# Fourteen idle matmuls in place of twelve, and a new hand-written order of work, in a kernel that mixes an FFT filter with a two-layer network

## The chip, the cores and the metric

The kernel runs on one core of one Trainium2 chip. The metric is the device time of one execution in microseconds (us). Before the change it is 129.68 us, the median of three runs (129.40, 129.68, 129.87). The engines are called PE or TensorE (matmuls), ACT or ScalarE, DVE or VectorE, POOL or GpSimd, and SP (which issues most DMAs here).

## What is computed

The input x has 2048 rows of 512 values in bf16. Three things are made of it:

```python
g = _sigmoid((x * gate_w).sum(-1, keepdims=True))   # one number for each row
a = irfft2(rfft2(x) * (w_r + 1j * w_i))             # a filter in two-dimensional frequency space
h = x @ w1 + b1                                     # 512 -> 1792
b = (h * tanh(softplus(h))) @ w2                    # Mish, then 1792 -> 512
return g * a + (1 - g) * b
```

The part with w1 and w2 is called the dense part below, the one with the FFT the spectral part.

## The kernel before

**Tasks.** `_build` doesn't loop over work and issue it. It makes a graph of 615 tasks (`G.add`, L175), each with an engine, a function that issues its instructions, what it reads and writes, and the PSUM banks that it takes and frees. `schedule` (L216) then reads the string `ORDER` (L258 to L274), which lists all tasks in one order: two digits in base 62 are a task's number (in the order of creation); where a task may run on several engines a letter chooses one (`v` VectorE, `a` ScalarE, `g` GpSimd); where it takes a PSUM bank one more digit names the bank (of eight). Each engine runs its own tasks in that order (`run_engine`, L842), strictly one after the other, and waits by semaphore for the tasks on other engines that a task depends on. A task that takes a bank depends on everything that read the bank's former content (L236 to L247). The constants in `PR`, the durations such as `mm`, `dve_dur`, `pool_dur` and the `tail` and `bw` of a DMA are the costs by which a planner made the string; when the kernel is built they choose nothing.

**Warm-up.** `warm0` to `warm15` (L423 to L429) are matmuls of a zeroed tile, which nobody reads: the first `NWARM` = 12 have 256 columns, the other `NFILL` = 4 have 128. They are tasks too; thirteen stand in front of the first transposes and three behind.

**Loads.** x comes in five DMAs on SP (`ld_x0`: tiles 0 and 1, `ld_x2`: tiles 2 and 3, then four tiles each). The first block of w1 comes in two halves, `ld_w1_0_0` and `ld_w1_0_1`, on the queue of ScalarE. All DMAs of SP go out in SP's order.

**Transposes.** `tr0a`, `tr0b`, `tr2a`, `tr2b` transpose two tiles of x and half of the columns each (four matmuls of 128 columns, L476), `tr4` to `tr14` two tiles (eight); `evx...` copy the result to xT.

**Dense part.** For each of four chunks of 512 rows (`c`) `mm1_c_ft` (L773, four matmuls of 512 columns) makes one of 14 blocks of h and `mish_c_ft` (ScalarE, L788) applies Mish. The first four blocks of chunk 0 are cut into quarters, `mm1a0_ft`, `mm1a1_ft`, `mm1b0_ft`, `mm1b1_ft`: `a` and `b` are the first and the last 256 rows, 0 and 1 the halves of w1 (two matmuls of 256 columns each). `mm2_t_0` and `mm2_t_1` (L803, seven matmuls of 512 columns each) make row tile t of b, and `bev_t` (L755 on ScalarE, L756 on VectorE) copies it out times 1 - g.

**Spectral part.** `ts`, `td` (VectorE) fold xT, `a10`, `a11` (L512) transform the rows, `eg` (ScalarE) and `e1p`, `e1m`, `e1f` combine, `s1` (L538) transforms the columns, `e2` copies out, `r1w` and `r1r` write it to memory and read it back in another layout. `s2` (L635), `wm` (VectorE), `wz` (GpSimd), `s2i` (L695) multiply by the filter; `e4`, `r2w`, `r2r` copy, write and read back. `s1i_t` (L723), the copy `e5_t` and `a1i_t` (L734; four matmuls of 128 columns each) transform back. From the bank of `a1i_t`, `gc_t` (ScalarE, L739) and then `sam_t` and `sap_t` (VectorE, L745) make sums and differences; these three free the bank. `sbm_t` and `sbp_t` (L751, `tt` at L408) add and subtract them, from SBUF to SBUF, on GpSimd; at the end `sum_t` (VectorE, L823, from SBUF to SBUF, L408 too) adds the dense and the spectral part, and an `out` DMA stores two tiles. Tiles 14 and 15 have `fin_t` (L815) in place of `sum_t`.

**Gate.** `gdot0` to `gdot15` (VectorE, L554), then `gpow` (GpSimd, L559), `gadd`, `gcol`, `omg` (VectorE).

Of the kernel before, what the change touches and what calls it, by code (L numbers as in the profile page):

```python
# [165 lines left out]
class _Graph:  # L166
# [89 lines left out]
DIGITS = "0123456789ABCDEFGHIJKLMNOPQRSTUVWXYZabcdefghijklmnopqrstuvwxyz"  # L256
ENGINE = {"p": "pe", "a": "act", "v": "dve", "g": "pool", "s": "sp"}
ORDER = (  # L258
    "020L0M0T0500O060N070P03080R090A0Q000B040C010S0D0E0F0U0G0V0H2y0w30W0y70I0J0xv0X0K6k50Y6z11046p00Z11a0a0zv1220b6"
    "u313v1G7701H711Jv6l0c6m721Iv6v736w6x6n6y1K40d7420e1M6o1L10f1461Nv750g1630h15v7670i1Ov1U40j1V27717v1850k1Pv0l1e"  # L260
    "v1W7810m1fv0n7A31Xv0o790p1Yv1A67B0q1C10r1Bv1Za1r70s1Dv1g41i0t19v7C20u2i7E37D20v7G62j7F6q21v1q47H1h26r1s1kv6s7I"
    "16t2k1la7K31jv7J2l7M47L1uv2322m7N2252D67a0241vv1tv1E126v7b25v27v7c37e07d1Fv2C72n7f1Q27g12E2Mv7i01Rv7h331a47j2G"
    "v7k11S1ba2Fv7m02Nv1T7l2Hv1m22o1c7n2O62Y71nv1d7o12Q2a2Z02p7q57p1o2cv1p2P11w32Rv7r7s62Sv1xa7u72dv2bv7t1y2822q7v2"
    "I41z29v7w12Ta2Ja2U62r7x2A7y32Vv2B2e17z2K8002s2fa2L8E62t2W818G72u2X8F2v2g8I58H2h2w8K18J2x8L2z8M2388O0398N3A8Q78"
    "P3B8S68R30318U1328T0v8V347358W4368Y2378X8a08Z3C38b3D63E8c53Mv8e18d3F3Qv3G7O08f3Pv7P3Lv3Sg3H23Y67Qa3I3Ng3Z43a7R"
    "23hv3Rg3b7S3c3mv3Og3d17U07Ta3e3J3iv3K3T7V3lv3jg3U43kg7Wa7X13Wa3Vv3ng3X3u63v23og7Y3w44v3f43v3g8s07Za3p3x48v3q44"
    "5g8t8u13sa3rv46g8w08v47v4G43t8x3y4H68y14Tv4Ag3z28208z4Pv49g834J404I4Qv414K424B9014Uv4Sg4L4922914M84v4N4C44Wg93"
    "8514Da4Ev4O4Vg4F864X4Rg94087a4Y4958814Za4av4b898B08Aa8C4c4d4e8g18Da4f963982979A0999C59B4g34o49D9E04hv4pa4i54w3"
    "9F5444q64xv4j8h55a4l4r4k4t5C04ng5K48ia4s4y55625Dv4mg5La5S38j15Tv4z4vg57514ug505E7595a453g5F5i3585U65ba8k5jv52g"
    "5V5G5Bg5X5H8m05Ag8la5W9av9bv5k59ev5M29c5l8n9dv5N5Ig9f5P5Jg5O8p18oa5Zg5m5n5Rg5c25q49gv5y55d6635Qg5ra5zv9G667a5f"  # L270
    "5pg6055e9H9I75Yg615s39hv8q9J635hg9i5t629jv5v5gg6E68ra5u6M49K764g6Nv6Fa9kv5xg9l6816U3699L5og6Vv6A5wg6B6c365g9Ma"
    "6W56G49N09nv6da9pv6H9mv6X6I6Dg9O9o6Z6Y6Cg6J6ag6O76e39Pa9Q29qv6f6bv9r6P6Lg6g6R9R6Kg6Q6h6Tg9U59sv9S6ig6jv9T9X16S"
    "g9V9W9tv9u9Y9Z"
)  # L274
NBF = 14
GD_N = 8
# [6 lines left out]
SPEC = (3, 4, 5, 6, 7)  # L283
DENSE = {0: (0, 1, 2, 3), 1: (0, 1), 2: (0, 1), 3: (0, 1)}
DENSE2 = {0: (0, 1), 1: (0, 1), 2: (0, 1), 3: (0, 1)}
NWARM = 12
NFILL = 4
PR = dict(tr=99.0, sp=95.0, mm1=88.0, mish=97.0, mm2=70.0, fin=98.0, gate=96.9, sum=98.5)

# [1 line left out]
def _build(nc, A_x, A_w_r, A_w_i, B_x, B_w1, B_b1, B_w2, gate_w, out):  # L291
# [8 lines left out]
    with es:  # L300
# [86 lines left out]
        def mm(n):  # L387
            return n / 2400.0 + 0.0025
# [10 lines left out]
        def pe(name, dur, fn, **kw):  # L399
            return G.add(name, "pe", dur, fn, lat=0.17, **kw)  # L400
# [21 lines left out]
        tw = []  # L422
        for i in range(NWARM + NFILL):  # L423
            n = 256 if i < NWARM else 128
            tw.append(pe(f"warm{i}", mm(n), lambda e, n=n: e.matmul(ps[:, pw.bank, 0:n], act[:, 2, 0, 0:128], act[:, 2, 0, 0:n], start=True, stop=True),  # L425
# [512 lines left out]
```

## Time and profile before

| | us |
|---|---|
| median of three runs | 129.68 |
| time of the profiled execution | 130.35 |
| its span, first to last instruction | 128.6 |
| TensorE busy | 123.2 |
| VectorE busy | 90.9 |
| ScalarE busy | 70.9 |
| GpSimd busy | 52.7 |

The difference between the span and the time of the same execution, 1.75 us, lies around the span. Busy time of TensorE has a peculiarity: matmuls are pipelined, so that the duration of one (0.379 us for 512 columns) is longer than the distance to the next (0.216). Where a row counts fewer instructions than the code issues, records are missing, and the profile shows the place as idle time.

### The profile page before, as it was taken

Reading aid. Unit: us, or ns where it says so; the run is one execution under the profiler, and the core shown is the slowest. Engines: PE = TensorE matmul, PEld = TensorE weight load, DVE = VectorE, ACT = ScalarE, POOL = GpSimd, SP = SyncE. Lnnn points to the kernel's source line nnn. Section 1 sums busy time; section 2 is a strip of 40 time slices with the busy share of each in tenths; the row PEclk is TensorE's granted clock in tenths of the full one; section 3 lists DMA queues with packets and bytes.
Section 4 is the critical chain, followed back from the end, with each engine's and each line's share of the span. In section 5 each row is a group of like instructions: output and inputs, shape, how many; then the busy total and the mean of one; then the engine's idle time right before and its main releaser. Section 6 shows DMA issues by size and latency. Waiting matters only on the chain.

```text
span 128.6 us, 2680 instructions
## 1 busy us (share of the span) xinstructions
PE 123.2 (96%) x1012; PEld 68.0 (53%) x1030; DVE 90.9 (71%) x173; ACT 70.9 (55%) x115; POOL 52.7 (41%) x83
## 2 busy tenths in 40 slices
PE   6999999999999999999999999999999999999992
PEld 4787756645544444444444444444466556555571
DVE  0255999998999711987679994300059999889992
ACT  1347768779898877522228415722597536735400
POOL 4000000001000266079897789200008977895770
PEclk9999999999999999999999999999999999999999
DMA  3999999999945559700040500555930012220313
GB/s 76 341 399 398 281 179 194 169 259 353 342 128 155 171 148 382 290 0 0 5 136 28 163 3 15 158 163 138 392 125 0 5 63 100 84 82 22 147 41 122
DMA packets 18509, 20.11 MB, mean 156 GB/s; under 512 B 1216, under 2 KB 15552, under 8 KB 18368
## 3 DMA queue, kind: packets, MB, share of 16 engines
q1 hardware_dynamic: 17648, 19.15, 49.9%
q10 hardware_dynamic: 816, 0.79, 1.9%
q8 instruction: 8, 0.13, 0.4%
q14 instruction: 5, 0.04, 0.1%
q0 software_dynamic: 32, 0.00, 0.0%
HBM read 13.64 MB, written 6.29 MB: 155 GB/s over the span
## 4 chain that ended last, share of the span: by engine, by line
PE 92%; DMA 3%; ACT 2%; issue 1%; DVE 0%
PE ps L773 38%; PE ps L803 37%; PE ps L476 3%; PE ps L723 3%; PE ps L512 3%; PE ps L734 3%; PE ps L538 3%; DMA xo<-in_A_x_dram 3%; ACT act L788 2%; PE ps L635 1%; ACT xo L755 1%; PE ps L695 0%; DVE xo L815 0%; PE ps L425 0%; PE ps L484 0%
## 5 line engine op out<-in xcount | busy, mean ns | idle before, releaser
L773 PE MATMUL ps<-xT,w_sb 128*128 128x512 bf16 (+1 forms) x231 | 52.5, 367 | 0.6 <-issue 0.2
L803 PE MATMUL ps<-w_sb,act 128*128 128x512 bf16 (+1 forms) x229 | 49.4, 366 | 0.9 <-ACT act L788 0.3
L788 ACT ACTIVATE act<-ps,b1f 128x512 bf16<-128x512 f32 x56 | 38.3, 687 | 17.2 <-PE ps L773 12.5
L803 PEld LDWEIGHTS ps<-w_sb,act 128*128 128x128 bf16 x238 | 22.3, 98 | 22.8 <-issue 0.8
L773 PEld LDWEIGHTS ps<-xT,w_sb 128*128 128x128 bf16 x240 | 22.6, 99 | 21.9 <-issue 0.6
L408 POOL TENSOR_TENSOR Tg<-Qb 128x256 bf16<-128x256 f32 x30 | 22.8, 791 | 20.7 <-DVE Qb L745 20.7
L408 POOL TENSOR_TENSOR Zb<-Qb 128x510 bf16<-128x510 f32 x16 | 20.0, 1268 | 4.7 <-DVE Qb L408 3.8
L755 ACT ACTIVATE xo<-ps,omg 128x512 bf16<-128x512 f32 x13 | 8.9, 687 | 22.9 <-PE ps L803 17.5
L408 DVE TENSOR_TENSOR Qb<-ps,WT 128x1024 f32<-128x1024 f32 x16 | 18.8, 1214 | 0.7 <-POOL Zb L408 0.7
L745 DVE SCALAR_TENSOR_TENSOR Qb<-ps,gcol,Qb 128x256 f32<-128x256 f32 x32 | 13.5, 474 | 0.7 <-POOL Tg L408 0.6
L403 DVE CAST Zb<-ps 128x512 bf16<-128x512 f32 x8 | 5.5, 689 | 11.9 <-PE ps L723 11.8
L403 DVE CAST Ybuf<-ps 128x1024 bf16<-128x1024 f32 x8 | 9.8, 1220 | 5.6 <-PE ps L695 5.1
L408 DVE TENSOR_TENSOR Abuf<-ps,Tg 128x512 bf16<-128x512 f32 x16 | 10.5, 682 | 2.1 <-PE ps L512 2.1
L576 POOL COPY wrv<-WT 128x32 bf16<-128x32 bf16 x2 | 0.4, 227 | 26.6 <-DMA WT<-in_A_w_i_dram 26.6
L554 DVE SCALAR_TENSOR_TENSOR Tg<-xo,Tg 128x512 bf16<-128x512 bf16 x16 | 10.9, 684 | 0.2
L739 ACT ACTIVATE Qb<-ps,gcol 128x256 f32<-128x256 f32 x16 | 7.1, 475 | 4.0 <-PE ps L734 4.0
L408 DVE TENSOR_TENSOR xo<-xo,Tg 128x512 bf16<-128x512 bf16 x14 | 9.1, 678 | 0.0
L403 DVE COPY xT<-ps 128x1024 bf16<-128x1024 bf16 (+1 forms) x9 | 5.2, 595 | 5.3 <-PE ps L476 5.3
L559 POOL TENSOR_TENSOR gcol<-omg,gdot 128x16 f32<-128x16 f32 x1 | 2.9, 2942 | 14.5 <-DVE Tg L554 14.5
L404 ACT ACTIVATE Ybuf<-ps 128x1024 bf16<-128x1024 f32 x8 | 8.2, 1021 | 0.1
L734 PE MATMUL ps<-GMs,Zb 128*128 128x128 bf16 x64 | 5.5, 219 | 0.0
L476 PE MATMUL ps<-ident,xo 128*128 128x128 bf16 x64 | 5.4, 236 | 0.1
(61 smaller groups left out, 84.2 us busy)
## 6 DMA issues: line engine op xcount, KB each, us to landing
Abuf<-scr SPq DMA_DIRECT2D x8, 512.0 KB, 5.6
scr<-Ybuf SPq DMA_DIRECT2D x16, 128.0 KB, 2.2
scr<-Ybuf SPq DMA_DIRECT2D x4, 512.0 KB, 2.9
w_sb<-in_B_w_dram SPq DMA_DIRECT2D x2, 896.0 KB, 12.7
out_dram<-xo SPq DMA_DIRECT2D x7, 256.0 KB, 2.0
xo<-in_A_x_dram SPq DMA_DIRECT2D x3, 512.0 KB, 7.6
rt<-c_rt SPq DMA_DIRECT2D x2, 512.0 KB, 8.8
WT<-in_A_w_r_dram SPq DMA_DIRECT2D x7, 128.5 KB, 11.0
```

The lines of the kernel that those rows point to most:

```text
L403: fs = {"dve": ("dve", dve_dur(n, rate=rate), lambda e: e.tensor_copy(out=dst(), in_=src())), "act": ("act", act_dur(n), lambda e: e.activ ...
L404: "act": ("act", act_dur(n), lambda e: e.activation(dst(), src(), AF.Copy))}
L408: f = lambda e: e.tensor_tensor(out=o(), in0=i0(), in1=i1(), op=op)
L476: ins = e.transpose(psb[:, pt.bank, o:o + 128], xo[:, t0 + i, d0:d0 + 255:2], ident[:, :])
L554: lambda e, t=t: e.scalar_tensor_tensor(out=junk, in0=xo[:, t, :], scalar=1.0, in1=gwb, op0=ALU.mult, op1=ALU.mult, accum_out=gdot[:, t:t ...
L734: ins = e.matmul(ps[:, p5.bank, 128 * i:128 * i + 128], TT[:, sl, 2 * par + ri, :], GMs[:, i, :], start=True, stop=True)
L739: lambda e, t=t, sl=sl, p5=p5: e.activation(gC[:, sl, :].rearrange("p (i n) -> p i n", i=2), ps[:, p5.bank, :].rearrange("p (i n) -> p i n ...
L745: lambda e, t=t, sl=sl, p5=p5, o=o, op=op: e.scalar_tensor_tensor(out=st1[:, sl, o::2, :], in0=ps[:, p5.bank, :].rearrange("p (i n) -> p i ...
L755: G.add_multi(f"bev_{t}", [("act", act_dur(512, True), lambda e: e.activation(xo[:, t, :], ps[:, pd.bank, :], AF.Copy, scale=omg[:, t:t + ...
L773: ins = e.matmul(ps[:, pd.bank, cols[0]:cols[1]], w1_sb[:, i, 128 * ft:128 * (ft + 1)], xT[:, i, 512 * c + cols[0]:512 * c + cols[1]], sta ...
L788: lambda e, ft=ft, pd=pd, hb=hb: e.activation(act[:, hb, ft, :], ps[:, pd.bank, :], AF.Mish, bias=b1f[:, ft:ft + 1]),
L803: ins = e.matmul(ps[:, pd.bank, cs_], act[:, hb, ft, 128 * tl:128 * (tl + 1)], w2_sb[:, ft, cs_], start=(ft == 0), stop=(ft == NFT - 1))
```

## The change

`NWARM` goes from 12 to 14 and the string is a new one:

```diff
 ORDER = (
-    "020L0M0T0500O060N070P03080R090A0Q000B040C010S0D0E0F0U0G0V0H2y0w30W0y70I0J0xv0X0K6k50Y6z11046p00Z11a0a0zv1220b6"
...
-    "g9V9W9tv9u9Y9Z"
+    "30020N0O000V0550Q060P070R080T09010A0S030B040C0U0D0E0F0W0G0H0X0I0J0y30Y1070K0Z11v0za0a0L1261406r20b0M15v6m16w51"
...
+    "vv9Z59X9uv9Y9w9a9b"
 )
...
-NWARM = 12
+NWARM = 14
```

There are 617 tasks now, the two new ones idle matmuls of 256 columns. All others are the same tasks with the same instructions, but for 28 copies and additions that have another engine, and for the banks. Read digit by digit, the two strings give these orders at the places that the prediction speaks of.

TensorE at the start, from the end of the warm-up:

```
before: warm11 warm12 tr0a tr0b warm13 warm14 warm15 mm1a0_0 mm1a0_3 tr2a mm1a0_1 tr2b mm1a0_2 tr_small mm1a1_3 ...
after:  warm13 warm14 tr0a tr0b warm15 warm16 tr2a tr2b mm1a0_1 warm17 mm1a0_0 mm1a0_2 tr_small mm1a0_3 mm1a1_2 ...
```

After the transform back has begun (the order after; banks in brackets where they are spoken of):

```
TensorE: s1i_3 a1i_0 a1i_2 a1i_1 mm2_7_1 s1i_4 s1i_5 a1i_3 mm2_8_0 a1i_5[6] mm2_8_1 mm2_9_0 a1i_4[6] s1i_6 s1i_7
         s1i_8 s1i_9 mm2_9_1 a1i_6 a1i_7 s1i_10[6] mm2_10_0
ScalarE: e5_0 e5_1 e5_3 gc_0 gc_1 gc_2 e5_4 gc_3 e5_5 gc_5 gc_4 e5_7 e5_9 bev_9
VectorE: sam_0 sap_1 sam_1 sap_2 sam_2 bev_7 sap_3 sam_3 sap_0 sam_5 sap_5 bev_8 sum_1 sum_0 sum_2 e5_6 sap_4 e5_8
         sam_4 sum_3 sap_7
GpSimd:  sbm_1 sbp_1 sbm_2 sbp_2 sbp_0 sbm_0 sbp_5 sbm_3 sbp_3 sbm_5 sbp_4 sbm_4
```

The same place before:

```
TensorE: a1i_0 s1i_2 s1i_3 a1i_1 mm2_8_1 s1i_4 s1i_5 a1i_2 a1i_3 s1i_6 mm2_9_0 a1i_4[7] s1i_7 s1i_8 a1i_6 mm2_9_1
         mm2_10_0 a1i_8[5] a1i_5 mm2_10_1 mm2_11_0 a1i_7 s1i_9 s1i_10[5]
VectorE: sam_0 sap_0 sam_1 sap_1 e5_4 e5_6 sam_2 sap_2 sam_3 sap_3 e5_8 sap_4 sam_6 sam_4 sap_6 sum_0 sum_1 sum_3
         sum_2 sam_5 sap_5 sap_8 sam_8 sum_4
GpSimd:  sbp_0 sbm_0 sbp_1 sbm_1 sbp_2 sbm_2 sbp_3 sbm_3 sbm_4 sbp_4 sbp_6 sbp_5
```

Elsewhere: `evx0a` goes from VectorE to ScalarE and `evx2a` the other way; `e4_01`, `e4_20` and `e4_30` go to VectorE, `e4_00`, `e4_21` and `e4_31` to ScalarE; on SP `r1w0a` goes in front of `ld_w2_1`, and `out7` in front of `out5`; on GpSimd `gpow` goes behind `wab1` and `wab2`; the `s1` tasks come earlier among the dense blocks (`s1_0` in front of `tr8`, `s1_14` in front of `mm1_1_10`), all of chunk 3's `mm1` comes before `s1i_0`, where blocks 11 to 13 came behind it, and `sbm_14`, `sbm_15` go to VectorE.

More of the change, by code (lines that the diff above doesn't have):

```diff
@@ L258 @@
 ORDER = (
-    "020L0M0T0500O060N070P03080R090A0Q000B040C010S0D0E0F0U0G0V0H2y0w30W0y70I0J0xv0X0K6k50Y6z11046p00Z11a0a0zv1220b6"
[L260 to L272, printed above, removed]
-    "g9V9W9tv9u9Y9Z"
+    "30020N0O000V0550Q060P070R080T09010A0S030B040C0U0D0E0F0W0G0H0X0I0J0y30Y1070K0Z11v0za0a0L1261406r20b0M15v6m16w51"
@@ new lines @@
+    "I07170c13v6x6n1J0d1Kv6y720e731Lv746o0f756s6p1M46q6t1W06z1O6u1N1163701Qv0g1876v0h1Pv7641Y0i19v0j1X17717v0k1av0l"
+    "0m7821Zv0n1gv0o7A0790p1hv1Ra0q7C57B1bv0r0s1S17D0t1A61Tv1t70u1i51s01j40v1k1Bv7E31u1U1mv7G10w7F1wv1V1na1C02k7H7I"
+    "61Dv1xa1lv7J22v1c17K31vv1da23v7M07L1e1E17N1f2l7O21Fv7c52m7P2531G02n7d2447e71Hv262Pv7g67f27v2E47h7i12Ov2G28v2F2"
+    "351o67j2Iv2Q529a2R47k32S1pv2Ja7m07l2Hv1q7o12Uv7n1r2o1y62Va7p2Tv7q01za2p3622A4377r2a3202K62Bv382c2b2217s12La392"
+    "ev2C7u02dv7t2D2W42fv2M7v2g62Xv2N7w12ha7y02q7x2Y8062r7z2Z2s8232i812t2j8G1832u8I08H2v8K38J3A2w8M43B8L2x3C8O72y8N"
@@ new lines @@
+    "3D2z8P0x8Q6318S18R8U48T8W08V3E2328X3F6333Nv8Y17Q03Ov8Z343G7R3Pg3H3Rv3Qg3Sv8a47Sa3a23I8b3b03Ug8c63kv8e73Tg3d8d3"
+    "nv3J58g48f3c3K3jv3e7T63L8h3M3V3ov3mg3W23f73Xa3Yv3lg7U3g3Z3qg3w47Va3x23h45v7W03pg3y46v3i7X3r4Av48g3s47Ya49v7Z14"
+    "7g3ua3tv4Bg7a3z3v4Cg4I37ba4J64Rv8u5404128414L8v4Sv4K42854Wv4Ug4Vv438w34M86a444Tg4N58y28x4O9044D8z4P4Yg92091941"
+    "4Q934Xg4E2959604Ga4Fv4Z986974H4a2999A14ca4bv9C79B4d8749D9E69G59F4e9I09H4f9K74g9J4h889L8A189v8B4i58Cv4q34ja4y28"
+    "D74zv4ra5634k157a5064s58E4l4t4n514u5E34v5M4525Fa5804wg8i553598Fv5Na4xg5A54g5O65B8j5P4m55g5R4pg5Q8l18kv4og9dv9c"
@@ L274 @@
+    "v5G65U49fv5H5c55k05Vv5Tg5s35da8m5I5ta5Cg5lv5Dg5J5W45e28na5Sg6069e8o05f9gv61a5Lg5g9h5X5h5Kg5u55Z5m66825v5Y5ig8p"
+    "5n69v5bg5w5o5jg8r15p8qa5x5ag9mv6G58s9lv6Ha5rg9n9iv6O75qg6I28ta6269M05zg6Pa639jv9ov9k6W1655yg6e36A46Xa646Q59N6B"
+    "9pv6R66g9q6D6J6C67g6fa6Y66S9P79Oa6T6Eg6L6Z6Vg6b6g56Fg6a9Q6h9rv6i6dg6K9S49sv9Rv6Ug9t6j9T6cv6kv6lv6Mg9W39U6Ng9V9"
+    "vv9Z59X9uv9Y9w9a9b"
 )
```

## Prediction

> **What bounds the kernel now.** I read the page's busy line and its chain first, then TensorE in order of time, then stretch by stretch.
>
> ```profile
> PE 123.2 (96%) x1012; PEld 68.0 (53%) x1030; DVE 90.9 (71%) x173; ACT 70.9 (55%) x115; POOL 52.7 (41%) x83
> ...
> PE 92%; DMA 3%; ACT 2%; issue 1%; DVE 0%
> ```
>
> TensorE is busy for 96% of the span and is 92% of the chain. Busy is not the same as unstalled, so I compared starts: a 512-column matmul starts 0.216 us after the one before, a 128-column one 0.056. From 7.6 to 126.1 us the starts follow each other at these steps, with 18 holes of 0.216 (or a little more), each of one matmul. The code issues 208 matmuls of 512 columns at L773 and 210 at L803; the rows by shape hold 199 and 201. So the 18 holes are missing records, and the chain's small ACT shares beside them are no waits. **After its start TensorE never waits**; each piece of work it has must be done, so the only thing a new order can win is in the first 7.6 us, and any new wait is paid in full.
>
> TensorE in order of time over the start (start, duration, instructions):
>
> ```profile
> 1.25 2.85 PE L425 MATMUL ps<-act 128*128 128x256 bf16 x13 [1.25 <-DVE act L417]
> 4.19 1.03 PE L476 MATMUL ps<-ident,xo 128*128 128x128 bf16 x8
> 5.02 0.53 PE L425 MATMUL ps<-act 128*128 128x128 bf16 x3
> ...
> 6.94 0.39 PE L476 MATMUL ps<-ident,xo 128*128 128x128 bf16 x4
> ```
>
> Eight transposes take 1.03 us from 4.19, four take 0.39 from 6.94 (each time with 0.16 to 0.21 of tail): the step is 0.107 in the first and 0.056 in the second. Between 6.62 and 6.83 TensorE goes from half rate to full; the page's PEclk row reads 9 throughout and doesn't show it. The first two tiles of x land at 4.14, the next two at 5.51, the second half of the first w1 block at 7.09.
>
> VectorE and GpSimd, at the first final additions (`sum_t`, L823) and the GpSimd additions (`sbm_t`, `sbp_t`, L751):
>
> ```profile
> 102.83 0.73 POOL L408 TENSOR_TENSOR Tg<-Qb 128x256 bf16<-128x256 f32 x1
> ...
> 102.88 2.70 DVE L408 TENSOR_TENSOR xo<-xo,Tg 128x512 bf16<-128x512 bf16 x3
> ...
> 103.52 1.77 POOL L408 TENSOR_TENSOR Tg<-Qb 128x256 bf16<-128x256 f32 x2
> ```
>
> Three sums take 2.70, 0.96 for the first and 0.87 to each further end; a sum with GpSimd idle takes 0.41 (minimum of its row). Each ends about 0.28 after the GpSimd addition under which it began: GpSimd ends at 103.56, 104.43, 105.29, the sums at 103.84, 104.71, 105.58. The two engines take turns, **0.87 a pair**.
>
> **The change, part by part.**
>
> *Two more idle matmuls.* At half rate a 256-column one takes 0.213. The warm-up ends at 3.89 now and would end at 3.89 + 2 x 0.213 = 4.32; the first transpose starts at 4.19 now: 0.13 later. Then eight transposes to 5.17 and two fillers to 5.38, and the second transposes (`tr2a`), moved in front of the first dense blocks, wait for 5.51 + 0.04 = 5.55: 0.17 idle, still at half rate. Eight transposes to 6.41, `mm1a0_1` over the change of rate to 6.78, one filler 0.06, four matmuls of 0.109 to 7.27, `tr_small` 0.21, two of 0.109: 7.70 when the same work is done that now ends at 7.59. **+0.11.** If x lands later than 4.32, or the full rate comes so early that both orders wait for w1 at 7.09, it is nothing; the other end is 0.2 (0.13 + half of 0.17).
>
> *Where the new order makes TensorE wait.* `s1i_10` takes bank 6, which `a1i_4` held, so it waits for the last reader, `sam_4` on VectorE. In VectorE's new queue, behind `bev_8`, stand `sum_1`, `sum_0`, `sum_2`, `e5_6`, `sap_4`, `e5_8`, `sam_4`. I count from the start of the last matmul of `mm2_8_1`, which `bev_8` waits for.
> TensorE up to `s1i_10`: that matmul and the 14 of `mm2_9_0` and `mm2_9_1`, 15 x 0.216 = 3.24; seven tasks of four (`a1i_4`, `s1i_6` to `s1i_9`, `a1i_6`, `a1i_7`), 28 x 0.056 = 1.56; it is free at **4.80**.
> VectorE: the result comes after 0.38, hand-over 0.03: `bev_8` starts at 0.41 and lasts 0.74 (row L756); the next instruction of this engine starts 0.08 before the end of one: 1.07. After the sums, `e5_6` and `e5_8` step by 0.61 (rows of 0.69), `sap_4` by 0.40, `sam_4` lasts 0.47, hand-over 0.04: 2.13 in all. With free sums, 3 x 0.34: 1.07 + 1.02 + 2.13 = 4.22, no wait.
> But GpSimd is then at work. Its first addition waits for `sam_1`. By the same counting back (25 x 0.056 + 20 x 0.216 = 5.71 from `a1i_0` to zero, then `e5_3` 0.60 and `gc_0` 0.47 on ScalarE, three VectorE steps) `sam_1` ends at -3.40, GpSimd begins at -3.37 and steps by 0.69 through ten additions whose inputs are there: the seventh runs 0.75 to 1.48, three more are queued. So `sum_1` ends at 1.48 + 0.28 = 1.76, `sum_0` at 2.63, `sum_2` at 3.50; less the 0.08 overlap, 3.42 + 2.13 = 5.55. **TensorE waits 5.55 - 4.80 = 0.75**, all on the path, as nothing behind `s1i_10` can pass it and TensorE has no idle time to take it up. The place of the seventh addition isn't sure: if one just ends at 1.07, `sum_1` takes 0.41 and the wait is 0.47; if one just begins, 1.07.
> [...]
>
> *What I cost at nothing*, with its cover. The dense blocks and the spectral stages that change places issue the same matmuls, and the eight switches to the partial-array shapes of L635 and L695 (some 0.09 each side) stay eight. `evx0a` goes from VectorE (0.43) to ScalarE (0.60): read 0.7 after it ends. On SP `r1w0a` passes `ld_w2_1`: its data (`e2_0`) are there before, and w2's second half lands at 35.1, is late by one issue of 0.6, and is read at 51. The round trip through memory starts earlier: the last `r1w` goes out at about 40.3 (42.8 now), the first `r1r` lands 6.5 later, near 46.9, and `s2_0` stands at 48.6. On GpSimd `gpow` (2.94) moves behind `wab2` and ends near 48.5; VectorE's `gadd` waits for it in front of `wm00`, which has to wait for `s2_0`, at 49.0, anyway. `e4_01` goes to VectorE (1.22 for 1.02): `s2_4` has 0.14 left. Laid on the same durations, other short margins are `s1_10` behind `e2_6` 0.15, `a10_4` and `a11_0` 0.18, `a1i_6` behind `e5_6` 0.21; without such cover each costs what it is late. The old order laid the same way has 0.09 and 0.10 at `s2i_1` and `s2_4`, where the trace shows no wait, so I trust them. The tail is the same: `fin_15_1` 0.48, then the last store.
>
> *Sum:* 0.11 + 0.75 = **+0.86**. The profiled execution took 130.35 (span 128.6, 1.75 around it) and would take 131.2 (span 129.5). It lies 0.67 above the median of 129.68; the difference goes onto the median: **130.5**.
>
> **The rivals.**
>
> *No new wait (ends not slower).* If GpSimd has caught up or is late when the three sums come, they cost 0.34 each, and there is 0.58 to spare at `s1i_10`; the wait decides from 0.58 of contention upward. For it: at 105.50 such a sum did take 0.41. Against: there GpSimd's queue had run dry waiting for `sam_5`, while here four additions are ready. Price: 129.68 + 0 to 0.15, so **129.75**; chance 0.17.
>
> *The full rate comes sooner (faster).* The two matmuls fill the idle 0.30 between 3.89 and 4.19. If that hole delays the change of rate, the new kernel has it by 4.3 and then waits for w1 only: 7.14 in place of 7.59, -0.45. Without the wait at `s1i_10` **129.2**, chance 0.08; with it 129.68 - 0.45 + 0.75 = 129.98, chance 0.05. Against: the rate changed 5.4 us after the first matmul in spite of the hole. [...]
>
> *A longer wait.* If a pair takes its two durations one behind the other, 0.41 + 0.73 = 1.14, `sum_1` ends at 1.48 + 0.41 = 1.89, `sum_2` at 4.17, and the wait is 4.17 - 0.08 + 2.13 - 4.80 = 1.42: 129.68 + 0.11 + 1.42 = **131.2**, and more if a margin of 0.14 to 0.21 fails too; chance 0.10. Against: 0.87 twice in the rows. [...]
>
> **How the numbers follow.** The forecast's case (wait 0.47 to 1.07, start 0 to 0.2) holds 0.60 and runs from 130.15 to 130.95; I say 130.5. A measurement of this kernel can tell 0.3%, 0.39 us, from no change (its three runs span 0.47). Slower than 130.07: 0.60 + 0.10 = 0.70. Within: 0.17 + 0.05 = 0.22. Faster than 129.29: 0.08. The range from 129.6 to 131.2 takes in the first rival and the forecast with the bounds above, and leaves out the fast end and most of the slow one.
>
> **What would show it.** Right: TensorE idle for 0.5 to 1.0 before an L723 matmul near 105 us, ended by VectorE's L745; the sums just before it at 0.7 to 1.0 each; the first L476 at 4.3. Wrong: no hole there and sums of 0.41; an L476 step of 0.056 before 6 us; or holes before L635, L695 or L538, which I excluded. The forecast falls first if GpSimd's additions start at another time than `sam_1` gives.

## The result, and the profile after

The changed kernel takes 130.94 us (median of four runs, 130.51 to 131.41) against 129.62; the ratio is 1.0102, interval 1.0054 to 1.0149. Taken again with six runs against 23 of the kernel before it is 1.0086 (1.0056 to 1.0115), 0.7 to 1.5 us slower.

The profiled execution took 131.41 us, its span is 129.7. The page's busy line and chain, after:

```profile
PE 123.9 (96%) x1015; PEld 68.4 (53%) x1032; DVE 91.0 (70%) x171; ACT 71.2 (55%) x118; POOL 51.8 (40%) x82
...
PE 87%; DVE 7%; issue 2%; ACT 1%; DVEq 0%
...
L723 PE MATMUL ps<-GMs,Abuf 128*128 128x128 bf16 x64 | 5.1, 219 | 0.7 <-DVE Qb L745 0.7
```

The busy share is still 96%, and so says nothing. What is new is that VectorE has 7% of the chain, and the last line, of the costliest groups: in front of an L723 matmul TensorE was idle for 0.7 us, until an L745 instruction of VectorE ended. In order of time, TensorE and then VectorE at that place:

```profile
104.42 0.61 PE L734 MATMUL ps<-GMs,Zb 128*128 128x128 bf16 x8
105.71 0.40 PE L723 MATMUL ps<-GMs,Abuf 128*128 128x128 bf16 x4 [0.69 <-DVE Qb L745]
106.16 0.59 PE L803 MATMUL ps<-w_sb,act 128*128 128x512 bf16 x2
```

```profile
100.48 0.75 DVE L756 TENSOR_SCALAR xo<-ps,omg 128x512 bf16<-128x512 f32 x1
101.15 2.52 DVE L408 TENSOR_TENSOR xo<-xo,Tg 128x512 bf16<-128x512 bf16 x3
103.60 0.68 DVE L403 CAST Zb<-ps 128x512 bf16<-128x512 f32 x1
104.20 0.47 DVE L745 SCALAR_TENSOR_TENSOR Qb<-ps,gcol,Qb 128x256 f32<-128x256 f32 x1
104.59 0.68 DVE L403 CAST Zb<-ps 128x512 bf16<-128x512 f32 x1
105.19 0.47 DVE L745 SCALAR_TENSOR_TENSOR Qb<-ps,gcol,Qb 128x256 f32<-128x256 f32 x1
```

This is the chain of the prediction: `bev_8`, three sums, `e5_6`, `sap_4`, `e5_8`, `sam_4`, which ends at 105.66; `s1i_10` starts at 105.71. The eight matmuls in front of it would have let it start at 104.86 (the last starts at 104.81, and the step is 0.056), so **the hole costs 0.85 us**. The profile's 0.69 is less, since it counts from the modelled end of the matmul before, not from where the next could start.

TensorE over the start, after:

```profile
1.25 3.27 PE L425 MATMUL ps<-act 128*128 128x256 bf16 x15 [1.25 <-DVE act L417]
4.32 1.06 PE L476 MATMUL ps<-ident,xo 128*128 128x128 bf16 x8
5.17 0.42 PE L425 MATMUL ps<-act 128*128 128x128 bf16 x2
5.38 1.06 PE L476 MATMUL ps<-ident,xo 128*128 128x128 bf16 x8
```

The first transpose starts at 4.32, not when x lands, and the second transposes find their x landed (5.30). The first step at full rate is at 7.18 here and was at 6.83 before.

The difference of the two spans adds up: `mm1a1` begins at 7.83 in place of 7.59 (0.24). From there to the start of `mm2_15_1` it is 117.66 in place of 116.81, 0.85, the hole alone. Together 1.09; the spans differ by 1.07.

### The profile page after: what moved, and what is told of

Same layout as the page of the kernel before. It is cut to its first block, busy times and chain, and to the rows that moved or that the text cites. A ratio compares the mean times of both kernels' runs of the same rounds, so it can differ in the third digit from the quotient of the medians.

```text
span 129.7 us, 2689 instructions
## 1 busy us (share of the span) xinstructions
PE 123.9 (96%) x1015; PEld 68.4 (53%) x1032; DVE 91.0 (70%) x171; ACT 71.2 (55%) x118; POOL 51.8 (40%) x82
## 3 DMA queue, kind: packets, MB, share of 16 engines
HBM read 13.64 MB, written 6.29 MB: 154 GB/s over the span
## 4 chain that ended last, share of the span: by engine, by line
PE 87%; DVE 7%; issue 2%; ACT 1%; DVEq 0%
PE ps L803 35%; PE ps L773 35%; PE ps L476 3%; PE ps L425 3%; PE ps L512 2%; PE ps L734 2%; PE ps L723 2%; PE ps L538 2%; DVE xo L408 2%; DVE Abuf L408 2%; PE ps L695 1%; PE ps L635 1%; ACT act L788 1%; DVE Zb L403 1%; DVE Tg L554 1%
## 5 line engine op out<-in xcount | busy, mean ns | idle before, releaser
L773 PE MATMUL ps<-xT,w_sb 128*128 128x512 bf16 (+1 forms) x232 | 51.5, 367 | 0.8 <-issue 0.3
L803 PE MATMUL ps<-w_sb,act 128*128 128x512 bf16 (+1 forms) x230 | 50.4, 366 | 0.4
L408 POOL TENSOR_TENSOR Tg<-Qb 128x256 bf16<-128x256 f32 x29 | 21.8, 783 | 23.2 <-DVE Qb L745 22.8
L745 DVE SCALAR_TENSOR_TENSOR Qb<-ps,gcol,Qb 128x256 f32<-128x256 f32 x32 | 13.7, 476 | 4.2 <-ACT Qb L739 3.3
L755 ACT ACTIVATE xo<-ps,omg 128x512 bf16<-128x512 f32 x9 | 6.2, 688 | 13.3 <-PE ps L803 13.2
L404 ACT ACTIVATE Zb<-ps 128x512 bf16<-128x512 f32 x12 | 7.0, 597 | 8.3 <-PE ps L723 8.3
L756 DVE TENSOR_SCALAR xo<-ps,omg 128x512 bf16<-128x512 f32 x5 | 3.7, 747 | 9.4 <-PE ps L803 9.3
L723 PE MATMUL ps<-GMs,Abuf 128*128 128x128 bf16 x64 | 5.1, 219 | 0.7 <-DVE Qb L745 0.7
```

The source lines that it names most:

```text
L404: "act": ("act", act_dur(n), lambda e: e.activation(dst(), src(), AF.Copy))}
L408: f = lambda e: e.tensor_tensor(out=o(), in0=i0(), in1=i1(), op=op)
L723: ins = e.matmul(ps[:, p4.bank, o:o + 128], T2r[:, 2 * t + c, par::2], GMs[:, 4, :], start=True, stop=True)
L745: lambda e, t=t, sl=sl, p5=p5, o=o, op=op: e.scalar_tensor_tensor(out=st1[:, sl, o::2, :], in0=ps[:, p5.bank, :].rearrange("p (i n) -> p i ...
L755: G.add_multi(f"bev_{t}", [("act", act_dur(512, True), lambda e: e.activation(xo[:, t, :], ps[:, pd.bank, :], AF.Copy, scale=omg[:, t:t + ...
L773: ins = e.matmul(ps[:, pd.bank, cols[0]:cols[1]], w1_sb[:, i, 128 * ft:128 * (ft + 1)], xT[:, i, 512 * c + cols[0]:512 * c + cols[1]], sta ...
```

## The experiments

The changed kernel again, the sums behind `sam_4` and the kernels with fourteen and twelve idle matmuls ran on one chip beside 23 runs of the kernel before, the other four on another beside 35. Between the two groups the ratios to the kernel before are compared, not the times.

### The changed kernel again

> The changed kernel once more, to narrow its ratio of 1.0102 (1.0054 to 1.0149) to the kernel before. My theory (0.79 us of waiting in front of s1i_10, 0.1 to 0.25 at the start): 130.5 to 130.7. Rival (the first four runs were typical: two near 130.55 and two near 131.35, so something else of about 0.8 us comes and goes): a median of 130.9 or two groups again. In the profile a hole of 0.75 to 0.85 in front of the L723 matmul near 105 us; the step of TensorE changes between 5 and 8 us, and the later it changes the longer the execution.

Measured: 131.07 us (130.60 to 131.43), ratio 1.0086 (1.0056 to 1.0115). The hole in front of `s1i_10` is 0.85 again, though this execution has the full rate from 3.99 us on and took 130.61. So the hole is constant, and about 0.8 us come and go with the change of rate, which the table at the end of this section takes up. The median is the rival's and not my 130.5 to 130.7, though the six runs don't fall into two clear groups, and the change at 3.99 lies outside the 5 to 8 that I had expected.

### The three sums behind sam_4

```diff
 VectorE:
-bev_8 sum_1 sum_0 sum_2 e5_6 sap_4 e5_8 sam_4 sum_3 sap_7 sam_7
+bev_8 e5_6 sap_4 e5_8 sam_4 sum_1 sum_0 sum_2 sum_3 sap_7 sam_7
```

> The changed kernel with sum_1, sum_0 and sum_2 moved behind sam_4 on VectorE, nothing else. My theory: the wait in front of s1i_10 is gone (sam_4 ends about 2.5 us sooner, 1.7 before s1i_10 could start), 0.75 to 0.8 us less than the changed kernel; what is left over the kernel before is the start, 0.1 to 0.25 us. Rival (the sums only move the contention, and a later matmul waits for them): less than 0.4 gained and a new hole behind s1i_11.

Measured: 130.56 us, ratio 1.0053 (1.0029 to 1.0077). My expectation failed and the rival's new hole came. The gain over the changed kernel, 0.5 us in the medians with overlapping intervals, lies between the two expectations; the holes account for 0.14 of it. TensorE and VectorE of this kernel:

```profile
106.04 0.61 PE L734 MATMUL ps<-GMs,Zb 128*128 128x128 bf16 x8
107.20 0.40 PE L723 MATMUL ps<-GMs,Abuf 128*128 128x128 bf16 x4 [0.55 <-DVE Qb L745]
```

```profile
103.87 2.48 DVE L408 TENSOR_TENSOR xo<-xo,Tg 128x512 bf16<-128x512 bf16 x4
106.28 1.25 DVE L745 SCALAR_TENSOR_TENSOR Qb<-ps,gcol,Qb 128x256 f32<-128x256 f32 x3
```

The hole at `s1i_10` is gone, but four sums in a row now hold up `sap_7` and `sam_7`, and `s1i_11`, which takes the bank of `a1i_7`, waits for them: 0.71 lost in place of 0.85. I had looked only at the task that was late and not at the next one in the same queue.

### Short additions on GpSimd

```diff
-                tt(f"sb{nm}_{t}", lambda o=o: o, lambda sl=sl: st1[:, sl, 0:2, :], lambda sl=sl: st1[:, sl, 2:4, :], op, 256,
+                w = 4 if t in (3, 5) else 128
+                tt(f"sb{nm}_{t}", lambda o=o, w=w: o[:, :, 0:w], lambda sl=sl, w=w: st1[:, sl, 0:2, 0:w], lambda sl=sl, w=w: st1[:, sl, 2:4, 0:w], op, 256,
```

> The changed kernel with GpSimd's four additions sbm_3, sbp_3, sbm_5 and sbp_5 cut from 128 to 4 columns of each block (the rest of tiles 3 and 5 is left out); VectorE's and TensorE's queues are untouched. My theory (VectorE and GpSimd take turns): the sums that stand behind them take 0.41 to 0.5 us in place of 0.78 to 0.95, and the wait in front of s1i_10 falls from 0.79 to nothing; 0.7 to 0.9 us less than the changed kernel. Rival (VectorE's queue is simply too long there, whatever GpSimd does): the sums keep 0.8 to 0.95 and the wait stays above 0.6.

Measured: 130.31 us, ratio 1.0014 (0.9995 to 1.0033), by the ratios 0.9 us less than the changed kernel. First GpSimd in the changed kernel (the additions that stand beside the three sums), then GpSimd, VectorE and TensorE of this one (VectorE issues the same instructions as in the changed kernel; some lines are one higher):

```profile
100.25 4.01 POOL L408 TENSOR_TENSOR Tg<-Qb 128x256 bf16<-128x256 f32 x5
```

```profile
100.81 1.05 POOL L408 TENSOR_TENSOR Tg<-Qb 128x8 bf16<-128x8 f32 x4
```

```profile
100.38 0.75 DVE L757 TENSOR_SCALAR xo<-ps,omg 128x512 bf16<-128x512 f32 x1
101.05 1.10 DVE L408 TENSOR_TENSOR xo<-xo,Tg 128x512 bf16<-128x512 bf16 x3
102.33 0.69 DVE L403 CAST Zb<-ps 128x512 bf16<-128x512 f32 x1 [0.19 <-PE ps L723]
```

```profile
104.31 0.61 PE L734 MATMUL ps<-GMs,Zb 128*128 128x128 bf16 x8
104.76 0.39 PE L723 MATMUL ps<-GMs,Abuf 128*128 128x128 bf16 x4
```

The three sums take 1.10 in place of 2.52, 0.42 each, and the CAST behind them now waits for TensorE, not the other way round. There is no hole in front of `s1i_10`. So **it is the turns with GpSimd that make VectorE's queue late**; its length alone isn't.

### bev_8 on ScalarE

```diff
-VectorE: sam_5 sap_5 bev_8 sum_1 sum_0 sum_2        ScalarE: gc_5 gc_4
+VectorE: sam_5 sap_5 sum_1 sum_0 sum_2              ScalarE: gc_5 bev_8 gc_4
```

> The changed kernel with bev_8, one copy of 0.74 us, on ScalarE (idle there from gc_5 to gc_4) in place of VectorE. My theory (the wait is the length of VectorE's queue in front of sam_4): sum_1 starts 0.82 sooner, under one more addition of GpSimd, sum_2 ends 0.68 sooner, and the wait in front of s1i_10 falls from 0.79 to 0.1; 0.6 to 0.7 us less than the changed kernel, 0.2 to 0.45 over the kernel before. Rival (as with the moved sums, the time comes back at s1i_11): 0.1 to 0.2 us gained, and a hole of 0.5 or more in front of a later L723.

Measured: 130.06 us, ratio 1.0013 (0.9994 to 1.0031). VectorE, then TensorE of this kernel:

```profile
100.02 2.67 DVE L408 TENSOR_TENSOR xo<-xo,Tg 128x512 bf16<-128x512 bf16 x3
102.61 0.68 DVE L403 CAST Zb<-ps 128x512 bf16<-128x512 f32 x1
```

```profile
104.11 0.61 PE L734 MATMUL ps<-GMs,Zb 128*128 128x128 bf16 x8
104.72 0.40 PE L723 MATMUL ps<-GMs,Abuf 128*128 128x128 bf16 x4
```

The sums are as slow as before, but start 0.8 sooner against TensorE's work, and the hole is 0.16 (the last of the eight starts at 104.50; the next could at 104.56, and does at 104.72). 0.1 was expected. Nothing comes back at `s1i_11`. By the ratios it is 0.9 us less than the changed kernel, where 0.6 to 0.7 was expected and the hole accounts for 0.69; the rest is within the intervals.

### Fourteen and twelve idle matmuls in either order

```diff
 # new order, two idle matmuls fewer in front of tr0a
-NWARM = 14
+NWARM = 12
```

> The changed kernel's order with twelve idle matmuls of 256 columns: two fewer in front of the first transpose. My theory: the first L476 starts when x has landed (3.95 to 4.2) and not at 4.32, which gains 0 to 0.15 us in all; the wait in front of s1i_10 stays at 0.75 to 0.85. Rival (the two added matmuls bring the full rate sooner): slower than the changed kernel by 0.3 us or more, with the change of step later. Second rival (the two matmuls are what costs the part beyond 0.86): 0.4 faster or more.

Measured: 130.73 us, ratio 1.0066 (1.0040 to 1.0091), hole 0.85. It lies 0.2% under the changed kernel's 1.0086, less than the intervals can tell. In its profile x landed late, at 4.28, so that the first L476 starts at 4.33 after a wait, not at 3.95 to 4.2.

```diff
 # old order, two idle matmuls more in front of tr0a
-NWARM = 12
+NWARM = 14
```

> The old order with fourteen idle matmuls in place of twelve. My theory: slower than the kernel before by 0 to 0.2 us, since the first transpose starts at 4.32; no wait later. Rival (filling the hole before the first transpose brings the full rate sooner): faster by 0.3 us or more, with the change of step 0.5 us or more sooner. Second rival (two more matmuls make it later): slower by 0.4 or more.

Measured: 130.01 us, ratio 1.0012 (0.9988 to 1.0037): 0.16 us slower, with an interval from 0.16 faster to 0.48 slower. The first transpose starts at 4.31, no wait later. Neither rival of either run came.

### The new order without both

The same as with `bev_8` on ScalarE, and:

```diff
-VectorE: sum_1 sum_0 sum_2 e5_6 ... sam_8 sam_9 sum_7
+VectorE: sum_1 sum_0 e5_6 ... sam_8 sam_9 sum_2 sum_7
-NWARM = 14
+NWARM = 12
```

> The same with sum_2 and its store behind sam_9 as well, and with twelve idle matmuls in place of fourteen: the new order with neither suspected cost. My theory: no wait of TensorE over 0.1 us behind the start; within 0.15 us of the kernel before, as both have the same work on TensorE and start when x lands. Rival (the rest of the new order costs something that I haven't found): 0.3 us or more over the kernel before with no hole in TensorE. Second rival (the new order's start is better): 0.3 or more under it.

Measured: 129.97 us, ratio 1.0004 (0.9984 to 1.0024), no hole over 0.1 behind the start. The new order with its one late queue mended is as fast as the old, and no faster: in either TensorE has the same work and no gap. It beats the kernel before by nothing that can be measured, and no version here does.

### Twenty idle matmuls

```diff
 # old order
-NWARM = 12
+NWARM = 20
```

> The old order with twenty idle matmuls, eight more than before. My theory (they only take TensorE's time once x has landed, 0.213 each at half rate and 0.109 at full; the change of rate comes when it comes): the first L476 at 5.0 to 5.6, and 0.3 to 0.8 us over the kernel before, more the later the rate changes. Rival (more work in front makes the full rate come sooner): no slower than the kernel before, and the change of rate before 5 us.

Measured: 130.64 us, ratio 1.0046 (1.0021 to 1.0071), 0.6 us slower, as my theory has it; the first L476 is at 5.15, where x had landed at 4.07. The rate changed before 5 us, as in the rival, but the kernel isn't faster. In the profiled execution the last four tiles of x landed at 16.33 (14.19 to 14.88 in the other nine), and TensorE lost 0.68 waiting for them, so that its span isn't a clean measure. Without this wait the span is 128.63, still 0.4 to 0.5 above those with the nearest changes of rate in the table below (128.12 and 128.27); whether x was late in the other nine runs of this kernel isn't known.

### When the rate changes

Every profile shows when TensorE first steps at full rate (0.056 for 128 columns, 0.109 for 256). Eight of the ten traces also hold a record of the moment from which the full clock was granted, at most 0.1 us earlier. The holes taken off the span are those above.

| kernel | idle matmuls | first full-rate step, us | full clock granted from, us | span | less its hole |
|---|---|---|---|---|---|
| changed, again | 14 | 3.99 | 3.97 | 128.88 | 128.03 |
| new order without both | 12 | 4.46 | none | 128.12 | 128.12 |
| old order, twenty | 20 | 4.77 | 4.68 | 129.31 | 128.63 |
| sums behind sam_4 | 14 | 5.74 | 5.64 | 128.98 | 128.27 |
| new order, twelve | 12 | 5.77 | none | 129.16 | 128.31 |
| bev_8 on ScalarE | 14 | 6.22 | 6.18 | 128.68 | 128.52 |
| old order, fourteen | 14 | 6.32 | 6.29 | 128.43 | 128.43 |
| short additions | 14 | 6.69 | 6.66 | 128.71 | 128.71 |
| before | 12 | 6.83 | 6.83 | 128.61 | 128.61 |
| changed | 14 | 7.18 | 7.16 | 129.68 | 128.83 |

Leave out the twenty. Then the last column rises with the time of the change, with no row more than 0.1 us out of order, whichever order of work it is and whether there are twelve or fourteen idle matmuls: 0.8 us between 3.99 and 7.18. With twelve it changes anywhere from 4.46 to 6.83 (three profiles), with fourteen from 3.99 to 7.18 (six); no effect of the number shows.

The records say one thing more. In the kernel before and in the changed kernel the full clock ends behind the last matmul, 122.88 us after it began. In the second profile of the changed kernel and in the old order with twenty it is still granted at the end of the span (mean granted clock 1.000), over 124 us after it began. The eight moments from which it was granted lie between 3.97 and 7.16, that is 2.72 to 5.91 us after the first matmul. No run shows what sets them, and I couldn't set them, so their part in the 0.8 us stays a thing that goes together in the profiles.

## Why the prediction was right

**What bounds the kernel: right.** TensorE has no gap to win back, and a new wait was paid in full: the stretch behind the start is 0.85 longer, as long as the hole.

**The new wait: right in its place, its cause and nearly in its size.** The prediction counted from the last matmul of `mm2_8_1`, at 100.06 in the trace. `s1i_10` free: 4.80 predicted, 4.80 measured. `bev_8` 0.41 and 0.42, `sum_1` 1.07 and 1.09. The seventh GpSimd addition 0.75 to 1.48, measured 0.87 to 1.59: that is the 0.1 which I had too little, as `sam_0` took 0.12 to follow `gc_0` and the first addition 0.08 to follow `sam_1`, each counted at 0.03. (The 5.71 of the prediction counts from where the result of `s1i_3` is there, which `e5_3` waits for, not from the first matmul of `a1i_0`; from that it is 5.88. The end it gives for `sam_1` is 0.07 off.) The sums' ends 1.76, 2.63, 3.50; measured 1.87, 2.74, 3.61: 0.87 each, 0.28 behind the addition's end. So 0.75 was mis-sized by 0.10 and is 0.85.

**The start: +0.11, not shown as such.** In the two profiles it is 0.24: the first transpose 0.13 later at half rate is 0.07 of it, a change of rate 0.35 later the other 0.17; the wait for `tr2a` (0.17 in the prediction) didn't come there, as x landed at 5.30. With the old order two more idle matmuls cost 0.16 us, with an interval from -0.16 to 0.48. The 0.24 of the two profiles lies above the upper bound of 0.2, through a change of rate that came 0.35 later by chance as far as the table shows; the runs neither confirm nor contradict 0 to 0.2 for the two matmuls themselves.

**What was costed at nothing was nothing**: no hole over 0.1 us at any of the margins of 0.14 to 0.21.

**The rivals.** No new wait: fell with the hole, and the short additions show what it would have been. The full rate comes sooner: the mechanism isn't borne out. The rate does come by 4.3 in the second profile of the changed kernel, whose span less the hole is then 0.58 under the one before, near the 0.45 that I had priced; but it also comes at 7.18 in the first, and with twelve idle matmuls at 4.46. What I had priced as an effect of the change varies from one execution to the next. A longer wait: fell; the pairs took 0.87 and not 1.14, as the sum ends 0.28, not 0.41, behind the addition. No run shows a pair that takes its two durations one behind the other.

**The total.** 0.86 predicted, 1.3 measured in the first four runs and 1.1 in the six later ones, interval 0.7 to 1.5. The hole and the start's bounds make 0.85 to 1.05, inside it; what is beyond can't be told from the scatter that goes with the change of rate in both kernels. The start's 0.11 in it was right, if at all, by luck: neither the wait of 0.17 nor the change of rate came there as I had counted them.

## What to carry to other kernels

Where one engine has no gap, lay the new queues of the others on measured durations and look for the first bank or buffer that is freed too late; a mean duration won't do for an operation that takes turns with another engine, as it is 0.41 or 0.95 here depending on the neighbour. Here such a wait was mended by shortening the queue (giving one of its tasks to an idle engine: a hole of 0.16 in place of 0.85), and not by pushing tasks to behind the late one: the next in the queue was late then, with a hole of 0.71. Two more idle matmuls in front of TensorE's work cost nothing that could be told (0.16 us, interval -0.16 to 0.48), eight more went with 0.6 us, and the profiles show no effect of their number on the time at which the full rate comes (4.46 to 6.83 with twelve, 3.99 to 7.18 with fourteen, 4.77 with twenty).

## What I had not expected of the hardware

The change to full rate came between 2.7 and 5.9 us after the first matmul in ten executions of kernels that begin alike, and the spans less their holes differ by 0.8 us with it, nearly as much as the change under study. The page's PEclk row reads 9 throughout in the eight profiles that have one, because the records of the granted clock begin with the change itself (at 6.83 in the kernel before, 7.16 in the changed one): on the page only the steps between short matmuls (0.107, then 0.056 for 128 columns) show it. The 58 runs of the kernel before beside the experiments spread from 129.41 to 130.54, a little more than that.

The turns of VectorE and GpSimd are as regular as a clock: of 92 sums in the ten profiles that began under an addition of GpSimd, 81 ended 0.28 to 0.29 us behind its end and eleven 0.30 to 0.32.
